# One sum of weight blocks in each group made by an adding DMA of the GpSimd queue instead of a VectorE add

## The chip, the cores and the metric

The kernel runs on one core of one Trainium2 chip. What counts is the device time of one execution in microseconds (us); lower is better. The kernel before is given as the median of three timed runs, and one more execution was taken by the hardware profiler. Engines are named as in the profile: PE is TensorE, PEld its weight loads, DVE is VectorE, ACT is ScalarE, POOL is GpSimd, and SP is SyncE, which here does nothing but issue DMAs.

## The reference

Attention with a tanh cap on the scores, and two feed-forward layers behind it, on 4 x 448 = 1792 tokens:

```python
scores = scale * np.matmul(q, k.transpose(0, 1, 3, 2))   # 4 batches, 12 heads, 448 x 64
scores = cap * np.tanh(scores / cap)
attn = softmax(scores) @ v                               # -> x, 1792 x 768
h = x @ moe_w_in                                         # 768 -> 2048
x = (h - np.tanh(h)) @ moe_w_out                         # 2048 -> 768
h = x @ moe2_w_in                                        # 768 -> 2048
out = (h * (1.0 / (1.0 + np.exp(-1.702 * h)))) @ moe2_w_out
```

The result is wanted with fp32 accuracy. TensorE multiplies in a shorter format (fp32r), so each fp32 operand is split into a high part (ACT casts it: `hi_act`, line L76) and a low part (DVE subtracts the high part from it: `lo_dve`, L88), and each product is made by three matmuls: high x high, high x low, low x high.

## The kernel before, in words

The tokens go through the feed-forward layers in two passes of two batches (896 tokens each). Both passes read the same weights, which lie in the chip's memory as blocks of 128 x 768 fp32 (384 KB): `single[n]` as plain fp32, and `kept[i]` already split. The first layer's input product of the second pass is `gemm_in(0)` (L779 to L791): 16 weight blocks, each with two spans of columns (512 and 384) and 18 matmuls a span. Behind each span `g_cubic` (L676) makes h - tanh h with a handful of ACT and DVE instructions (L680 to L698).

The first layer's output product of the second pass is `gemm_out_seven` (L833, matmuls at L854), and the second layer's input product is `gemm_in_seven` (L913, matmuls at L938). They split the matrices in two halves each way and make seven block products instead of eight, so some of their weight blocks are sums of blocks: s1 = r21 + r22, s3 = r21 - r11, s2 = r22 + r21 - r11, s4 = r12 - s2. These sums are made in the second pass while `gemm_in(0)` and then `gemm_out_seven` run, written to the chip's memory (`side_a`, `side_i`), and read back as weight blocks. The last stage is `gemm_rows_seven` (L971, matmuls at L997 and L1018).

The sums are made by two generators, in steps that end at each `yield`. `sums_a` (L333) has KQ = 4 groups of four blocks of 128 x 768; each group takes both buffers of `wd_p` (`four_of_pairs`), with four loads (L338), four adds (`add`, L313, through `first_sums`, L322) and four stores (L342). `sums_i` (L347) has KH = 8 groups, each with one buffer, two loads of 384 KB (L351), four adds on halves of 128 x 384, and two stores (L357). In the program of the trace their tiles are named `pair`.

The order of the work is that in which the program is written, with a scheduler that lets an instruction go ahead by its priority. `ahead(i)` is called once per weight block: it prepares the block that is used LEAD = 2 blocks later (`prepare` and `fetch`, loads at L258 and L283), and it advances the generators by `rate` steps, which carries over. In the second pass:

```python
side.extend((sums_a(), sums_i()))
rate[0] = 2.25
yield from gemm_in(0)
until("a")
rate[0] = 0.5
gemm_out_seven()
until("i")
gemm_in_seven()
```

All the loads and stores named so far are issued by SP, one after the other, in the order of the program. Weight blocks of `gemm_in(0)` come as two DMAs straight from `kept` (`wh` and `wl`, L283); those of `gemm_out_seven` and `gemm_in_seven` come as fp32 (`whole`, L258), ACT casts the high part, and DVE makes the low part `wl`. There are three buffers for split weight blocks. GpSimd has its last instruction before the second pass.

Of the kernel before, what the change touches and what calls it, by code (L numbers as in the profile page):

```python
# [15 lines left out]
ALU = mybir.AluOpType  # L16
# [21 lines left out]
def attention_moe_moe(ctx, tc, q, k, v, cap, w_in1, w_out1, w_in2, w_out2, out):  # L38
    nc = tc.nc
# [13 lines left out]
    HW = DM // 2  # L53
# [84 lines left out]
    A0, I0, R0 = KF, 2 * KF, 3 * KF  # L138
    KQ = KF // 4
# [80 lines left out]
    KH = KF // 2  # L220
    SEVEN_A = ("11", "s2", "12", "s3", "s1", "s4", "22")
    SEVEN_B = ("11", "21", "22", "t2", "t3", "t1", "t4")
    single = [dr_p.tile([P, WC], F32, name=f"single{n}") for n in range(NCH - A0)]
# [88 lines left out]
    def add(out, a, kind, b):  # L312
        nc.vector.tensor_tensor(out=out, in0=a, in1=b, op=kind)  # L313

    def four_of_pairs():
        slots = []
        for _ in range(2):
            t = wd_p.tile([P, WC, 2], U32, tag="wd", name="pair").rearrange("p w t -> p (w t)").bitcast(F32)
            slots += [t[:, :WC], t[:, WC:]]
        return slots  # L320

    def first_sums(r11, r12, r21, r22):  # L322
        add(r22, r21, ALU.add, r22)
        yield "s1", r22
        add(r21, r11, ALU.subtract, r21)
        yield "s3", r21
        add(r11, r22, ALU.subtract, r11)
        yield "s2", r11
        add(r12, r12, ALU.subtract, r11)
        yield "s4", r12  # L330
# [3 lines left out]
    def sums_a():  # L334
        for j in range(KQ):
            r = four_of_pairs()
            for n, t in enumerate(r):
                nc.sync.dma_start(out=t, in_=single[n * KQ + j])  # L338
                if n % 2:
                    yield  # L340
            for m, t in first_sums(*r):
                nc.sync.dma_start(out=side_a[m][j], in_=t)  # L342
                yield
        done.add("a")

    def sums_i():
        for j in range(KH):  # L347
            t = wd_p.tile([P, WC, 2], U32, tag="wd", name="pair").rearrange("p w t -> p (w t)").bitcast(F32)
            r = t[:, :WC], t[:, WC:]
            for n in range(2):  # L350
                nc.sync.dma_start(out=r[n], in_=single[I0 - A0 + n * KH + j])  # L351
            yield
            for n, _ in enumerate(first_sums(*(x[:, a:a + HW] for x in r for a in (0, HW)))):
                if n == 1:
                    yield
            for n in range(2):
                nc.sync.dma_start(out=side_i[j][n], in_=r[n])  # L357
            yield
        done.add("i")
# [745 lines left out]
    def moe(b0):  # L1105
        if b0 + NB == B:
# [8 lines that stand above are left out]
        else:  # L1115
            yield from gemm_in(0)
            gemm_out()
            plain[0] = True
            open_plain()
            side.append(sums_b())  # L1120
            rate[0] = 2.0
            yield from gemm_in(1)
        gemm_rows_seven(b0)
# [59 lines left out]
```

## Time and profile before

| what | value |
|---|---|
| time, median of 3 runs | 1097.28 us (1093.85 to 1097.44) |
| profiled execution, span of the trace | 1094.2 us |
| PE busy | 1081.3 us, 99% of the span |
| DVE busy | 929.8 us, 85% |
| ACT busy | 668.7 us, 61% |
| POOL busy | 59.1 us, 5% |
| DMA | 220.58 MB, mean 202 GB/s |
| `gemm_in(0)`, `gemm_out_seven`, `gemm_in_seven` of the second pass | 113.80, 104.16 and 104.16 us of PE |

The profiled execution is known by its span, from the first instruction to the last. The median of the three timed runs is 3.1 us above that span, and the fastest run 0.3 us below it. "Busy" counts instructions that compute; the time in which an engine issues DMAs or waits is not in it. The DMA share is the mean over the core's 16 DMA engines.

### The profile page before, as it was taken

Reading aid. Unit: us, or ns where it says so; the run is one execution under the profiler, and the core shown is the slowest. Engines: PE = TensorE matmul, PEld = TensorE weight load, DVE = VectorE, ACT = ScalarE, POOL = GpSimd, SP = SyncE. Lnnn points to the kernel's source line nnn. Section 1 sums busy time; section 2 is a strip of 40 time slices with the busy share of each in tenths; the row PEclk is TensorE's granted clock in tenths of the full one; section 3 lists DMA queues with packets and bytes.
Section 4 is the critical chain, followed back from the end, with each engine's and each line's share of the span. In section 5 each row is a group of like instructions: output and inputs, shape, how many; then the busy total and the mean of one; then the engine's idle time right before and its main releaser. Section 6 shows DMA issues by size and latency. Waiting matters only on the chain.

```text
span 1094.2 us, 16108 instructions
## 1 busy us (share of the span) xinstructions
PE 1081.3 (99%) x5579; PEld 887.0 (81%) x5579; DVE 929.8 (85%) x1467; ACT 668.7 (61%) x1022; POOL 59.1 (5%) x56
## 2 busy tenths in 40 slices
PE   9999998999999999999999999999999999999998
PEld 3333333688998888899899998889999999999998
DVE  4688999799997787889897885999999898889775
ACT  6898888799893433445245654767645554455453
POOL 0013443200000000000000000000000000000000
PEclk9999999999999999999999999999999999999999
DMA  6767786465537989889835768888555333333344
GB/s 142 206 187 199 192 234 192 148 209 173 188 116 265 318 305 332 292 287 313 285 110 170 227 201 276 313 287 291 183 192 176 107 123 102 102 110 107 119 144 142
DMA packets 156466, 220.58 MB, mean 202 GB/s; under 512 B 58672, under 2 KB 108640, under 8 KB 156384
## 3 DMA queue, kind: packets, MB, share of 16 engines
q1 hardware_dynamic: 155088, 218.94, 62.9%
q8 instruction: 44, 0.72, 0.3%
q10 hardware_dynamic: 1296, 0.61, 0.2%
q14 instruction: 38, 0.31, 0.1%
HBM read 160.83 MB, written 58.68 MB: 201 GB/s over the span
## 4 chain that ended last, share of the span: by engine, by line
PE 85%; DMA 6%; DVE 5%; ACT 2%; issue 2%; SPq 1%; ACTq 0%; DVEq 0%
PE ps_h L791 32%; PE ps_o L1018 15%; PE ps_h L938 10%; PE ps_y L854 10%; PE ps_pv L498 7%; PE ps_sc L457 5%; DMA wd<-in_moe_w_out_dram 4%; PE ps_o L997 3%; DVE wr L185 1%; DVE wd L175 1%; PE ps_qk L436 1%; PE ps_r L505 1%; PE ps_tl L467 1%; PE ps_y L816 1%; ACT wr L168 1%
## 5 line engine op out<-in xcount | busy, mean ns | idle before, releaser
L791 PE MATMUL ps_h<-xh,wh 128*128 128x384 f32 (+1 forms) x576 | 184.5, 365 | 0.3 <-ACT xh L76 0.3
L791 PE MATMUL ps_h<-xl,wh 128*128 128x384 f32 (+1 forms) x576 | 183.8, 364 | 0.0
L791 PE MATMUL ps_h<-xh,wl 128*128 128x384 f32 (+1 forms) x576 | 131.4, 362 | 0.1
L76 ACT CAST rh<-gr 128x384 fp32r<-128x384 f32 (+1 forms) x141 | 73.7, 528 | 82.8 <-PE ps_o L1018 36.4
L791 PEld LDWEIGHTS ps_h<-xh,wh 128*128 128x128 f32 x576 | 107.1, 188 | 13.8 <-ACT xh L76 1.0
L791 PEld LDWEIGHTS ps_h<-xl,wh 128*128 128x128 f32 x576 | 107.0, 188 | 11.9
L76 ACT CAST wh<-whole 128x768 fp32r<-128x768 f32 (+1 forms) x105 | 84.9, 810 | 50.4 <-PE ps_h L938 30.9
L791 PEld LDWEIGHTS ps_h<-xh,wl 128*128 128x128 f32 x576 | 104.6, 188 | 13.4 <-issue 1.4
L1018 PE MATMUL ps_o<-wl,rh 128*128 128x384 f32 x336 | 112.4, 335 | 1.1 <-DVE wl L88 1.1
L1018 PE MATMUL ps_o<-wh,rh 128*128 128x384 f32 x336 | 112.3, 334 | 0.0
L1018 PE MATMUL ps_o<-wh,rl 128*128 128x384 f32 x336 | 112.3, 334 | 0.0
L88 DVE TENSOR_TENSOR wl<-whole,wh 128x768 fp32r<-128x768 f32 (+1 forms) x105 | 96.5, 921 | 9.4 <-ACT wh L76 7.8
L168 ACT ACTIVATE wr<-wd 128x768 f32<-128x768 f32 x64 | 57.9, 909 | 69.6 <-DMA wd<-in_moe_w_out_dram 41.2
L88 DVE TENSOR_TENSOR rl<-gr,rh 128x384 fp32r<-128x384 f32 (+1 forms) x141 | 79.8, 573 | 13.7 <-ACT rh L76 12.9
L476 ACT ACTIVATE t<-ps_sc,tsc 128x896 f32<-128x896 f32 x72 | 70.0, 1008 | 26.6 <-PE ps_sc L457 26.6
L175 DVE TENSOR_SCALAR wd<-wd 128x768 uint16<-128x768 uint16 x57 | 59.5, 1044 | 24.9 <-ACT wr L168 24.7
L478 ACT ACTIVATE t<-t,cpos 128x896 f32<-128x896 f32 x72 | 72.5, 1044 | 0.4
L816 PE MATMUL ps_y<-gh,wh 128*128 128x512 f32 (+1 forms) x192 | 70.0, 365 | 1.6 <-DVE xl L88 1.4
L816 PE MATMUL ps_y<-gl,wh 128*128 128x512 f32 (+1 forms) x192 | 69.9, 364 | 0.0
L457 PE MATMUL ps_sc<-qk 64*128 64x448 f32 x288 | 68.2, 572 | 0.8 <-ACT qk L76 0.6
L498 PE MATMUL ps_pv<-t,rv 128*64 128x448 f32 x288 | 64.2, 551 | 3.9 <-ACT t L476 3.4
L1018 PEld LDWEIGHTS ps_o<-wl,rh 128*128 128x128 f32 x336 | 63.1, 188 | 1.6 <-DVE wl L88 1.4
(145 smaller groups left out, 2307.6 us busy)
## 6 DMA issues: line engine op xcount, KB each, us to landing
wd<-in_moe_w_in_dram SPq DMA_DIRECT2D x64, 384.0 KB
wd<-in_moe_w_out_dram SPq DMA_DIRECT2D x32, 768.0 KB
single<-wr SPq DMA_DIRECT2D x48, 384.0 KB
whole<-single SPq DMA_DIRECT2D x43, 384.0 KB
pair<-single SPq DMA_DIRECT2D x40, 384.0 KB
s<-pair SPq DMA_DIRECT2D x32, 384.0 KB
whole<-s SPq DMA_DIRECT2D x32, 384.0 KB
wh<-kept SPq DMA_DIRECT2D x25, 384.0 KB
```

The source lines that it names most:

```text
L76: pin(nc.scalar.copy(out=dst, in_=src))
L88: pin(nc.vector.tensor_tensor(out=dst, in0=src, in1=hi.bitcast(F32), op=ALU.subtract))
L175: pin(nc.vector.tensor_scalar(out=half[:, :, 2], in0=half[:, :, 1], scalar1=F64_LOW, scalar2=None, op0=ALU.mult))
L457: pin(nc.tensor.matmul(ps[:, j, :S], qk[a, kc], qk[a, :S], start=True, stop=True))
L476: pin(nc.scalar.activation(out=t, in_=ps[:, :, :S], func=AF.Tanh, scale=tsc))
L478: ins = pin(nc.scalar.activation(out=tt[g, c], in_=tt[g, c], func=AF.Exp, scale=cpos))
L498: pin(nc.tensor.matmul(ps[a, :S], w, t[:, j], start=(c == 0), stop=(c == KC - 1)))
L791: pin(nc.tensor.matmul(ps, w[:, kk, :], x[kk][:, a], start=(m == 0), stop=(m == len(seq) - 1)))
L816: nc.tensor.matmul(bank[e][:, :a1 - a0], w[:, kk, c], x[2 * j + kk][:, a0:a1], start=(j == 0 and m == 0), stop=(j == KF // 2 - 1 and m == ...
L854: nc.tensor.matmul(ps[e], w[:, kk, c], x, start=(k == 0 and m == 0), stop=(k == KH - 1 and m == 2))
L938: nc.tensor.matmul(ps, w, x, start=(m == 0), stop=(m == len(seq) - 1))
L1018: nc.tensor.matmul(ps[n], x[:, t], w[:, kk, :], start=(k == 0 and m == 0), stop=(k == KH - 1 and m == 2),)
```

## The change

The add that makes s1 is taken out of `first_sums`. In its place, a DMA that GpSimd issues reads r21 once more from the chip's memory and adds it to r22 in the tile where r22 has just been loaded. In `sums_a` this DMA has a step of its own: one `yield` more per group. In `sums_i` it shares the step of the loads. The other three sums of a group stay on DVE, and the stores stay on SP.

```diff
     def first_sums(r11, r12, r21, r22):
-        add(r22, r21, ALU.add, r22)
         yield "s1", r22
         add(r21, r11, ALU.subtract, r21)
         yield "s3", r21
@@ sums_a
                 nc.sync.dma_start(out=t, in_=single[n * KQ + j])
                 if n % 2:
                     yield
+            nc.gpsimd.dma_start(out=r[3], in_=single[2 * KQ + j], accum_op=ALU.add)
+            yield
             for m, t in first_sums(*r):
                 nc.sync.dma_start(out=side_a[m][j], in_=t)
                 yield
@@ sums_i
             for n in range(2):
                 nc.sync.dma_start(out=r[n], in_=single[I0 - A0 + n * KH + j])
+            nc.gpsimd.dma_start(out=r[1][:, HW:], in_=single[I0 - A0 + KH + j][:, :HW], accum_op=ALU.add)
             yield
```

So 4 DVE adds of 128 x 768 and 8 of 128 x 384 go, and 4 DMAs of 384 KB and 8 of 192 KB come on the GpSimd queue. The steps of `sums_a` go from 24 to 28.

The order of the SP queue around the first group of `sums_a`, before (`pair` is a block of the group in its buffer, `s1_0` to `s4_0` are the group's sums in memory, `wh` and `wl` are weight blocks of `gemm_in(0)`):

```order
L338 DMA pair_6514<-single12_198 128x768
L283 DMA wh_6573<-kept3_173 128x768
L283 DMA wl_6574<-kept3_173 128x768
L283 DMA wh_6645<-kept4_174 128x768
L342 DMA s1_0_234<-pair_6514 128x768
L342 DMA s3_0_242<-pair_6514 128x768
L283 DMA wl_6646<-kept4_174 128x768
L342 DMA s2_0_238<-pair_6513 128x768
L342 DMA s4_0_246<-pair_6513 128x768
L283 DMA wh_6717<-kept5_175 128x768
L283 DMA wl_6718<-kept5_175 128x768
```

The same place on SP after the change:

```order
L337 DMA pair_6514<-single12_198 128x768
L283 DMA wh_6573<-kept3_173 128x768
L283 DMA wl_6574<-kept3_173 128x768
L283 DMA wh_6643<-kept4_174 128x768
L283 DMA wl_6644<-kept4_174 128x768
L343 DMA s3_0_242<-pair_6514 128x768
L343 DMA s1_0_234<-pair_6514 128x768
L343 DMA s2_0_238<-pair_6513 128x768
L283 DMA wh_6715<-kept5_175 128x768
L283 DMA wl_6716<-kept5_175 128x768
L343 DMA s4_0_246<-pair_6513 128x768
```

The stores of the first group stand later against the weight loads by one or two places; the store of s1 now stands behind that of s3, and ahead of the weight block `kept5`.

The order on DVE at the third group of `sums_a`, before, with the semaphores that each instruction waits on (DMAHW: a DMA of SP, DMASW: a DMA of GpSimd); the rows with `pair` are the four adds of the group, s1, s3, s2 and s4:

```order
L313 TENSOR_TENSOR pair_6872<-pair_6872 128x768 [waits DMAHW6_49,DMAHW3_49,DMAHW0_49]
L695 TENSOR_TENSOR g_t_6974<-g_v_6988,g_t_6974 128x512 [waits DVE_49,Activation_49]
L313 TENSOR_TENSOR pair_6872<-pair_6871,pair_6872 128x768 [waits DMAHW1_49,DVE_49]
L697 SCALAR_TENSOR_TENSOR gr6_4258<-gr6_4258,g_t_6974 128x512 [waits DVE_49,Activation_49]
L681 TENSOR_TENSOR g_far_7006<-ps_h_6978,g_t_7005 128x384 [waits Activation_49]
L698 COPY_PREDICATED gr6_4258<-g_m_6989,g_far_6975 128x512 [waits DVE_49]
L313 TENSOR_TENSOR pair_6871<-pair_6872,pair_6871 128x768 [waits DMAHW4_49]
L695 TENSOR_TENSOR g_t_7005<-g_v_7029,g_t_7005 128x384 [waits DVE_49,Activation_49]
L313 TENSOR_TENSOR pair_6871<-pair_6871 128x768 [waits DMAHW2_49,DVE_49]
```

The same place on DVE after the change (s3, s2, s4):

```order
L313 TENSOR_TENSOR pair_6940<-pair_6939,pair_6940 128x768 [waits DMAHW5_49,DMAHW7_49,DMAHW1_49,DMAHW0_49]
L697 TENSOR_TENSOR g_t_6970<-g_v_6984,g_t_6970 128x512 [waits DVE_49,Activation_49]
L699 SCALAR_TENSOR_TENSOR gr6_4258<-gr6_4258,g_t_6970 128x512 [waits DVE_49,Activation_49]
L700 COPY_PREDICATED gr6_4258<-g_m_6985,g_far_6971 128x512 [waits DVE_49]
L683 TENSOR_TENSOR g_far_7002<-ps_h_6974,g_t_7001 128x384 [waits Activation_49]
L697 TENSOR_TENSOR g_t_7001<-g_v_7023,g_t_7001 128x384 [waits DVE_49,Activation_49]
L313 TENSOR_TENSOR pair_6939<-pair_6940,pair_6939 128x768 [waits DMAHW4_49,DMAHW3_49,DMASW2_49]
L699 SCALAR_TENSOR_TENSOR gr6_4258<-gr6_4258,g_t_7001 128x384 [waits DVE_49,Activation_49]
L88 TENSOR_TENSOR rl6_4289<-gr6_4258,rh6_4288 128x448 [waits Activation_49]
L700 COPY_PREDICATED gr6_4258<-g_m_7024,g_far_7002 128x384 [waits DVE_49]
L313 TENSOR_TENSOR pair_6939<-pair_6939 128x768 [waits DMAHW2_49]
```

The add of s1 is gone; the add of s2 waits for the adding DMA (DMASW2) and stands five instructions behind that of s3. In the first group of `sums_a` six instructions stand between the two.

The order on SP at the loads of the eighth and last group of `sums_i` (`single23` and `single31`), before, where they stand among the weight loads in the middle of `gemm_out_seven`:

```order
L357 DMA s31_6_263<-pair_8186 128x768
L351 DMA pair_8386<-single23_209 128x768
L357 DMA s24_6_262<-pair_8186 128x768
L258 DMA whole_8096<-s3_3_245 128x768
L351 DMA pair_8386<-single31_217 128x768
L258 DMA whole_8124<-s1_0_234 128x768
```

The same loads after the change, among the weight loads of the beginning of `gemm_in_seven` (`s31_1`, `single25`):

```order
L258 DMA whole_8714<-s31_1_253 128x768
L352 DMA pair_8618<-single23_209 128x768
L352 DMA pair_8618<-single31_217 128x768
L258 DMA whole_8752<-single25_211 128x384
L258 DMA whole_8784<-single18_204 128x768
L359 DMA s31_7_265<-pair_8618 128x768
L359 DMA s24_7_264<-pair_8618 128x768
```

They have moved behind the whole of `gemm_out_seven`, with the group's adds on DVE. On PE nothing moves.

## Rows read from the trace of the kernel before

**Rows 1.** The page: the span, and each engine's busy time and instructions.

```profile
span 1094.2 us, 16108 instructions
PE 1081.3 (99%) x5579; PEld 887.0 (81%) x5579; DVE 929.8 (85%) x1467; ACT 668.7 (61%) x1022; POOL 59.1 (5%) x56
...
POOL 0013443200000000000000000000000000000000
```

**Rows 2.** The chain that ended last, in order: start us, length us, what.

```profile
660.22 4.01 DMA wl<-kept
...
664.27 113.80 PE ps_h L791 x564
778.07 104.16 PE ps_y L854 x504
882.23 104.16 PE ps_h L938 x504
```

**Rows 3.** Stretches: length, busy PE, PEld, DVE, ACT, POOL, PE clock, DMA share, GB/s.

```profile
680.00:700.00 20.00, 20.00 (x102) 18.09 (x101) 19.04 (x32) 14.39 (x25) 0.00 (x0) 1.00 0.87 302
700.00:720.00 20.00, 20.00 (x101) 18.09 (x101) 17.32 (x29) 13.38 (x24) 0.00 (x0) 1.00 0.83 291
720.00:740.00 20.00, 20.00 (x99) 17.80 (x98) 19.27 (x34) 14.13 (x25) 0.00 (x0) 1.00 0.89 310
740.00:760.00 20.00, 20.00 (x100) 17.82 (x99) 20.00 (x40) 13.16 (x22) 0.00 (x0) 1.00 0.92 312
760.00:780.00 20.00, 20.00 (x103) 18.28 (x102) 20.00 (x37) 15.71 (x26) 0.00 (x0) 1.00 0.61 216
780.00:800.00 20.00, 20.00 (x98) 18.18 (x97) 20.00 (x36) 11.07 (x20) 0.00 (x0) 1.00 0.54 182
```

**Rows 4.** DVE's groups from 664 to 850 us: busy us, mean ns, idle before.

```profile
L313 DVE TENSOR_TENSOR pair<-pair 128x384 f32<-128x384 f32 x32 | 17.2, 543 | 0.0
L313 DVE TENSOR_TENSOR pair<-pair 128x768 f32<-128x768 f32 x16 | 15.2, 950 | 1.4 <-DMA pair<-single 1.4
L698 DVE COPY_PREDICATED gr<-g_m,g_far 128x512 f32<-128x512 uint16 x16 | 11.8, 735 | 0.5
...
L697 DVE SCALAR_TENSOR_TENSOR gr<-gr,g_t 128x512 f32<-128x512 f32 x16 | 10.9, 684 | 0.6
```

**Rows 5.** Timeline of SP's queue: start us, time in the queue us, line, operation.

```profile
666.98 2.03 SPq L338 DMA_DIRECT2D pair<-single  x4
...
683.17 1.69 SPq L283 DMA_DIRECT2D wh<-kept  x1
...
705.81 0.42 SPq L338 DMA_DIRECT2D pair<-single  x1
```

**Rows 6.** Timeline of DVE, adds of sums_a; in brackets the wait ahead.

```profile
677.78 0.94 DVE L313 TENSOR_TENSOR pair<-pair 128x768 f32<-128x768 f32 x1
...
712.33 0.96 DVE L313 TENSOR_TENSOR pair<-pair 128x768 f32<-128x768 f32 x1 [1.44 <-DMA pair<-single]
```

**Rows 7.** Timeline of DVE, low parts of gemm_out_seven's second, third and fourth weight block.

```profile
771.61 0.94 DVE L88 TENSOR_TENSOR wl<-whole,wh 128x768 fp32r<-128x768 f32 x1
...
778.93 0.94 DVE L88 TENSOR_TENSOR wl<-whole,wh 128x768 fp32r<-128x768 f32 x1
...
782.96 0.94 DVE L88 TENSOR_TENSOR wl<-whole,wh 128x768 fp32r<-128x768 f32 x1
```

**Rows 8.** PE's waits from 600 us to the end: total us, times, longest.

```profile
PE ps_o L1018 <- DVE wl L88: 1.1, 1, 1.1
```

**Rows 9.** ACT's waits from 650 to 860 us: total us, times, longest.

```profile
ACT g_t L680 <- PE ps_h L791: 27.5, 19, 12.6
```

## The prediction

> **What bounds the kernel now.** I read the page first: PE is busy 1081.3 us of a span of 1094.2 us [rows 1], so at most 12.9 us could be won without taking work from PE, and the change takes none from it. Next comes the chain of waits, for the stages in which the sums are made: three PE blocks stand end to end, 664.27 + 113.80 = 778.07, and 778.07 + 104.16 = 882.23 [rows 2]. In such a chain a step from one PE block straight to the next means that PE went from matmul to matmul and nothing else came last. PE's own list of waits agrees: from 600 us to the end it has one wait, 1.1 us, and that one is in the last stage [rows 8]. The windows from 680 to 800 us show the same, 20.00 of 20 us PE at the full granted clock, and beside it a DVE that is nearly full: 19.04, 17.32, 19.27, and then 20.00 three times [rows 3]. So the change works on an engine that is close to the limit but not the limit. It can win nothing where PE never waits; the question is whether DVE, which now waits for GpSimd's DMAs, gets late enough that PE stops.
>
> **How late DVE may get.** DVE makes the low part `wl` of each weight block of `gemm_out_seven`, and PE needs it. That stage has 28 blocks in 104.16 us, 3.72 us a block [rows 2]. The third block is wanted at 778.07 + 2 x 3.72 = 785.51 and its `wl` was done at 778.93 + 0.94 = 779.87, 5.6 us early; the fourth at 789.23, done at 782.96 + 0.94 = 783.90, 5.3 us early [rows 2, 7]. These are the tightest margins, since before 778 the weights come split from memory and DVE has only h - tanh h to make; what DVE leaves undone there falls due from 778 on. So three things pay for waits before about 780 us:
> - the adds that go: 4 x 0.950 + 4 x 0.543 = 6.0 us [rows 4] (4 more of 0.543 go later);
> - DVE's idle time from 680 to 740: 0.96 + 2.68 + 0.73 = 4.4 us [rows 3];
> - the margin of `wl`: 5.3 us.
>
> Together 15.7 us. ACT is not the next limit: it waits for PE (27.5 us in 19 waits), not PE for it [rows 9].
>
> **What the change adds, part by part.**
> - *DVE.* 12 adds go, 4 x 0.950 + 8 x 0.543 = 8.1 us [rows 4]. Covered by PE, so worth nothing by themselves.
> - *The new wait.* The add for s2 now waits for the adding DMA, and this DMA may start only when r22 has landed. Queued behind the waiting add on DVE are the `g_cubic` instructions, and behind them `wl`. Let A be the time from the last load of a group having landed to the adding DMA having landed. No row shows such a DMA. From below, the one plain DMA of a block on the chain, 4.01 us [rows 2]. From above 13 us: a block load that was issued at 705.81 held DVE until 712.33 [rows 5, 6], 6.5 us in a busy stretch, and twice that for a DMA that has to read two sides and whose descriptors are written by a program. I take 4.0 + 1.3 = 5.3 us, the plain DMA and a second reading of 393 KB at the 312 GB/s that the busiest stretch moved [rows 3]; it is nearest to the row of 4.01 us, because that row is the same transfer between the same places.
> - *What of A is covered.* DVE doesn't go straight from the load to the s2 add: the order shows six instructions between the adds for s3 and s2 in the first group, five in the third. DVE's instructions there take 75.6 us over 135, 0.56 us each [rows 3]. First group: loads issued 666.98 to 669.01 [rows 5], landed by 675.5 with 6.5 us each; the first add of the group at 677.78 [rows 6], which with s1 gone is the place of s3, and six instructions end at 677.78 + 0.94 + 3.4 = 682.1, so 6.6 us of A are covered. Third group, the only one whose loads DVE waited for (1.44 us [rows 4, 6]): the last load landed at 712.33; DVE, no longer waiting, would do s3 at 710.9 and reach s2 at 710.9 + 0.95 + 2.8 = 714.6, so 2.3 us are covered. With A = 5.3 the stalls are 0 and 3.0 us, 1.5 in the mean.
> - *The sum.* At most eight adding DMAs are waited for before 780 us (four of `sums_a`, the first four of `sums_i`): 8 x 1.5 = 12 us against 15.7. The other four lie some 22 us apart in `gemm_out_seven`, and each has the margin of 5.3 us for itself. PE doesn't stop: 0 us.
> - *SP's queue.* The store of s1 now waits for the adding DMA, and behind it in SP's order stands the weight block `kept5`. It was issued at 683.17 [rows 5] and is wanted at 664.27 + 5 x 7.11 = 699.8 (16 blocks in 113.80 us [rows 2]), so with 6.5 us for its flight it may go at 693. The adding DMA of the first group has landed by 675.5 + 13 = 688.5 even at the upper bound. If that cover went, a block late by the difference would stop PE once. No effect.
> - *POOL.* It does nothing after the first quarter [rows 1]; its DMAs queue only behind one another.
> - *DMA.* Four more reads of 393 KB before 740 us are 1.57 MB, and each touches the destination too, so 5 us at 312 GB/s, up to 10 with the second side. The DMA share is 0.83 to 0.92 from 680 to 760 [rows 3], which leaves 0.13 + 0.17 + 0.11 + 0.08 = 0.49 of 20 us, 9.8 us. It fits, narrowly.
> - *The moved group.* The eighth group of `sums_i` goes from the middle of `gemm_out_seven` to the first blocks of `gemm_in_seven`: its two loads, three adds (1.6 us) and two stores stand there beside that stage's own loads. Its sums are used last of all, a whole stage later. Between 780 and 800 the DMA share has fallen to 0.54 [rows 3], so SP's loads have room. No effect, and if the cover is gone, one block late by about A - 5.3.
>
> The sum is the profiled span with nothing taken off or put on, 1094.2 us; the median of the shown runs lies 3.1 us above that span, so I forecast 1097 us.
>
> **The rivals.**
> - *DVE's waits stop PE (slower).* With the two covers the waits come to 8 x ((A - 6.6) + (A - 2.3)) / 2, a term below nothing counted as nothing. They pass 15.7 us at A = 6.2 us: that is the point from which it decides, and only 0.9 us above my value. For it speaks that block loads in this stretch took 6.5 us; with the second reading that is 7.8 us, which gives 4 x (1.2 + 5.5) - 15.7 = 11 us, so 1108 us. At the upper bound of 13 it gives 4 x (6.4 + 10.7) - 15.7 = 53 us, 1150 us. Against it: the load of 6.5 us had to get through SP's and the engines' queues together with three others, while the adding DMA goes out alone.
> - *The adding DMA doesn't start while DVE works (slower).* Then nothing of A is covered, since it begins only when DVE stands still for it: 8 x 5.3 - 15.7 = 27 us, 1124 us. It decides if DVE's instructions there hold GpSimd off. What DVE runs in this stretch are two-operand adds, predicated copies and the like [rows 4], and POOL's own work shows no such hold, because it has none there [rows 1]. The Trainium skill ("SBUF — State Buffer", section "SBUF: two separate sides") describes such a hold: descriptors of a GpSimd DMA can't be written while VectorE runs an instruction in a mode that takes the port pair which the two share. It names copies and the like for it, and no run here shows it.
> - *SP or the moved group makes a weight block late (slower).* One stop, at the price of an adding DMA that lands at 13 instead of 5.3: 8 us, 1105 us. For it: a store that waits stands ahead of weight loads. Against it: the margin of 4.5 us at the upper bound, worked out above.
> - *DVE's relief reaches PE (faster).* Were PE's blocks stretched by waits too short to be listed, 6.0 us less of DVE work could give up to 6 us, 1091 us. Against it: full windows and a single wait of 1.1 us [rows 3, 8].
>
> That the change doesn't do what it says is excluded by the order: the adds are gone and the DMAs are there.
>
> **How the numbers follow.** About 0.5% (5.5 us) is what a measurement of this kernel can tell from no change. My forecast, no change, has 0.68: it holds for A up to 6.2 us, and some way above it, since the first few us past it lie within 0.5%. The rivals: waits on DVE 0.20, the held-off DMA 0.05, a late weight block 0.03, so slower 0.28; DVE's relief, faster, 0.04. Low end 1092, the fastest run shown (1093.85) less 2 us for what of the relief may reach PE. High end 1110: it takes in the wait rival up to A = 8 and the late block; beyond it lie the upper half of the first rival and the second, together some 0.17.
>
> **What would show it.** Right: the three PE blocks are again 113.8, 104.2 and 104.2 us, PE has no wait between 664 and 1000 us, and DVE shows idle time before the `pair` adds of about 1.5 us a group, released by a GpSimd DMA. Also right: DVE's busy time is 8 us less, the new DMAs take 4 to 6 us from issue to landing. Wrong: PE waits for `wl` near 780 us, or for a `kept` block near 700 us; DVE stands for over 2 us at each s2 add; or the adding DMAs take over 6.2 us.

## The result and the profile after

The changed kernel takes 1104.42 us (median of 4 runs, 1102.09 to 1105.47), the kernel before 1095.73 us beside it (median of 4). The ratio is 1.0085, with a 95% interval of 1.0059 to 1.011: slower by 0.85%, 8.7 us. The time lies in the range given (1092 to 1110), but the forecast was no change, and that was wrong.

The page of the profiled execution, with its span and busy times (compare [rows 1]):

```profile
span 1103.6 us, 16143 instructions
PE 1080.6 (98%) x5579; PEld 888.2 (80%) x5579; DVE 922.9 (84%) x1455; ACT 666.5 (60%) x1022; POOL 69.6 (6%) x68
```

PE and ACT do the same work, DVE is busy 6.9 us less, and the span is 9.4 us longer: PE stands. The windows say where (columns as in [rows 3]: length, busy PE, PEld, DVE, ACT, POOL, PE clock, DMA share, GB/s):

```profile
680.00:700.00 20.00, 20.00 (x100) 17.89 (x99) 14.93 (x24) 13.19 (x24) 0.87 (x1) 1.00 0.86 266
700.00:720.00 20.00, 20.00 (x102) 18.09 (x101) 15.74 (x25) 11.93 (x22) 0.86 (x1) 1.00 0.85 286
720.00:740.00 20.00, 20.00 (x102) 18.07 (x101) 14.39 (x23) 10.45 (x19) 0.86 (x1) 1.00 0.74 251
740.00:760.00 20.00, 18.00 (x81) 15.48 (x80) 14.44 (x26) 9.42 (x17) 1.61 (x2) 0.91 0.84 246
760.00:780.00 20.00, 18.70 (x91) 16.18 (x90) 15.87 (x32) 9.78 (x17) 1.85 (x3) 1.00 0.85 269
780.00:800.00 20.00, 14.36 (x61) 11.68 (x60) 20.00 (x36) 15.09 (x27) 1.73 (x2) 0.91 0.71 210
800.00:820.00 20.00, 19.80 (x96) 17.67 (x95) 20.00 (x36) 11.08 (x21) 0.00 (x0) 1.00 0.47 151
```

Where before PE was busy 20.00 of 20 in each, it now loses 2.00 + 1.30 + 5.64 + 0.20 = 9.1 us, 3.3 of it before 780 us and 5.8 behind. (That 9.1 is so close to the 9.4 us of the span is chance: the last section has the rest of the sum.) DVE, nearly full before, has 4 to 6 us of idle time in each window up to 780 and is full only then.

PE's waits from 600 us to the end (total us, times, longest), where before there was one of 1.1 us [rows 8]:

```profile
PE ps_y L856 <- DVE wl L88: 3.1, 4, 1.0
PE ps_y L856 <- ACT wh L76: 2.8, 2, 2.1
PE ps_h L793 <- DMA wh<-kept: 2.6, 2, 2.0
PE ps_o L1020 <- DVE wl L88: 1.5, 1, 1.5
PE ps_h L793 <- DVE pair L313: 0.7, 1, 0.7
PE ps_o L999 <- DVE wl L88: 0.6, 1, 0.6
```

So there are two kinds of stop: in `gemm_in(0)` (L793) PE waits mostly for weights that come straight from memory (`wh<-kept`), which no DVE instruction makes, and in `gemm_out_seven` (L856) for the two parts of a weight block that ACT and DVE make. ACT's part (`wh`) is late by DVE too: up to 800 us ACT has no wait for the load of a `whole` block, but its casts stand in order behind its instructions of `g_cubic`, and these wait for DVE 26.8 + 17.6 us, against 11.3 + 2.8 before:

```profile
ACT g_m L696 <- DVE gr L700: 26.8, 13, 4.8
ACT g_v L693 <- DVE g_t L697: 17.6, 10, 5.2
```

DVE's groups of `pair` adds from 664 to 850 us (busy, mean ns, idle before; compare [rows 4]):

```profile
L313 DVE TENSOR_TENSOR pair<-pair 128x768 f32<-128x768 f32 x12 | 11.4, 954 | 14.4 <-DMA pair<-single 14.4
L313 DVE TENSOR_TENSOR pair<-pair 128x384 f32<-128x384 f32 x21 | 11.4, 548 | 7.6 <-DMA pair<-single 7.6
```

DVE now waits 22.0 us ahead of these adds, against 1.4 before. For the third group, GpSimd's queue and then DVE (start us, us, engine, line, operation, wait ahead):

```profile
717.04 0.86 POOL L340 DMA_DIRECT2D pair<-single  x1 [20.53 <-DMA wl<-kept]
```

```profile
722.87 0.96 DVE L313 TENSOR_TENSOR pair<-pair 128x768 f32<-128x768 f32 x1 [3.76 <-DMA pair<-single]
```

The adding DMA is issued at 717.04, and DVE's add for s2, which waited 3.76 us for it, starts at 722.87, 5.8 us later. (The bracket on GpSimd's row names a weight load; where a wait is for several semaphores, the profile names one of them. The load that the adding DMA waits for has landed at 716.4.) The view of DMA issues (count, KB each, median us from issue to landing) has 5.5 and 4.8 us for the two sizes:

```profile
pair<-single POOLq DMA_DIRECT2D x4, 384.0 KB, 5.5
pair<-single POOLq DMA_DIRECT2D x8, 192.0 KB, 4.8
```

Of the 22.0 us, 19.2 lie in six waits for adding DMAs (1.9 to 4.1 us each), and 2.8 in two waits for plain loads that came late.

The chain that ended last (start us, length us) is no longer PE's alone, as in [rows 2]. From 717 to 790 us it runs through the groups of sums: an adding DMA, the store of a sum, the loads of a next group, its adding DMA, and at last DVE's `wl`:

```profile
717.04 5.80 DMA pair<-single
...
726.20 2.69 DMA s<-pair
728.95 7.67 DMA pair<-single
...
738.15 5.19 DMA pair<-single
...
753.72 5.88 DMA pair<-single
...
767.39 3.50 DMA s<-pair
771.32 6.99 DMA pair<-single x2
...
789.83 0.88 DVE wl L88
790.75 4.82 PE ps_y L856 x15
...
893.56 102.14 PE ps_h L940 x504
```

The rows at 717.04, 738.15 and 753.72 start with GpSimd's issues: they are adding DMAs.

SP's queue stands too. First its longest waits from 662 to 800 us before (total us, times, longest). Those at L258 and L283, ended by a weight buffer's becoming free, are the time by which SP is early with weight loads, 41.3 us in all; this is called SP's lead below. The others are stores that wait for DVE's adds:

```profile
SPq L258 <- DVE wl L88: 21.5, 7, 6.3
SPq L342 <- DVE pair L313: 21.0, 15, 4.1
SPq L283 <- PE ps_h L791: 19.8, 14, 5.4
SPq L357 <- DVE pair L313: 14.5, 9, 2.8
```

The same stretch after the change:

```profile
SPq L343 <- DMA pair<-single: 23.2, 4, 6.7
...
SPq L359 <- DMA pair<-single: 14.7, 3, 6.5
...
SPq L283 <- PE ps_h L793: 6.4, 4, 4.9
...
SPq L258 <- DVE wl L88: 5.8, 1, 5.8
```

The stores of the sums (L343, L359) now hold SP 37.9 us for the adding DMAs, and still 25.0 us for DVE (19.2 and, at L359, 5.8), where before they held it 35.5 us for DVE. The lead falls from 41.3 to 12.2 us.

### The profile page after: what moved, and what is told of

It reads as the page before. It is cut to its first block, busy times and chain, and to the rows that moved or that the text cites. A ratio compares the mean times of both kernels' runs of the same rounds, so it can differ in the third digit from the quotient of the medians.

```text
span 1103.6 us, 16143 instructions
## 1 busy us (share of the span) xinstructions
PE 1080.6 (98%) x5579; PEld 888.2 (80%) x5579; DVE 922.9 (84%) x1455; ACT 666.5 (60%) x1022; POOL 69.6 (6%) x68
## 4 chain that ended last, share of the span: by engine, by line
PE 81%; DMA 8%; DVE 5%; ACT 2%; issue 2%; SPq 1%; DVEq 0%; ACTq 0%; POOLq 0%
PE ps_h L793 26%; PE ps_o L1020 14%; PE ps_h L940 9%; PE ps_y L856 9%; PE ps_pv L500 7%; PE ps_y L818 5%; PE ps_sc L459 5%; DMA pair<-single 3%; PE ps_o L999 2%; DMA wd<-in_moe_w_out_dram 2%; PE ps_qk L438 1%; PE ps_r L507 1%; PE ps_tl L469 1%; DVE wd L175 1%; ACT t L478 1%
## 5 line engine op out<-in xcount | busy, mean ns | idle before, releaser
L793 PE MATMUL ps_h<-xh,wh 128*128 128x384 f32 (+1 forms) x576 | 185.3, 367 | 3.3 <-DMA wh<-kept 2.6
L793 PE MATMUL ps_h<-xl,wh 128*128 128x384 f32 (+1 forms) x576 | 184.7, 366 | 0.0
L793 PE MATMUL ps_h<-xh,wl 128*128 128x384 f32 (+1 forms) x576 | 131.3, 362 | 0.0
L793 PEld LDWEIGHTS ps_h<-xh,wh 128*128 128x128 f32 x576 | 107.7, 189 | 17.4 <-DVE g_t L697 2.3
L793 PEld LDWEIGHTS ps_h<-xl,wh 128*128 128x128 f32 x576 | 107.5, 189 | 12.2
L793 PEld LDWEIGHTS ps_h<-xh,wl 128*128 128x128 f32 x576 | 104.7, 188 | 12.9 <-issue 1.4
L175 DVE TENSOR_SCALAR wd<-wd 128x768 uint16<-128x768 uint16 x57 | 59.6, 1045 | 23.4 <-ACT wr L168 23.2
L856 PE MATMUL ps_y<-rh,wl 128*128 128x448 f32 x168 | 62.6, 373 | 3.1 <-DVE wl L88 3.1
```

The costliest lines, as they stand in the source:

```text
L175: pin(nc.vector.tensor_scalar(out=half[:, :, 2], in0=half[:, :, 1], scalar1=F64_LOW, scalar2=None, op0=ALU.mult))
L793: pin(nc.tensor.matmul(ps, w[:, kk, :], x[kk][:, a], start=(m == 0), stop=(m == len(seq) - 1)))
L856: nc.tensor.matmul(ps[e], w[:, kk, c], x, start=(k == 0 and m == 0), stop=(k == KH - 1 and m == 2))
```

## The experiments

Two theories stood at first. D: DVE's standing makes the low parts `wl` of the weight blocks late. S, later widened to C: the adding DMA is a serial link in the chain of a group (loads, adding DMA, adds, stores, next loads into the same buffer), and SP, which issues that chain in order with the weight loads, gets late with these. The kernel before was timed beside each run on the same chip; its medians were 1094.0 to 1094.3 us. "Stop" is what PE's busy time lacks in the profile, in `gemm_in(0)` and in `gemm_out_seven`; "DVE waits" are its idle times ahead of `pair` adds; "backlog" is explained below the table. The medians are of 4 to 12 executions, while stops, waits and backlog are those of one profiled execution of each kernel, so the two need not agree to the last us.

| run | median us | ratio (95%) | stop, `gemm_in(0)` | stop, `gemm_out_seven` | DVE waits for `pair`, to 800 us | backlog |
|---|---|---|---|---|---|---|
| the change | 1104.42 | 1.0085 (1.0059 to 1.011) | 3.3 | 5.8 | 22.0 | 14.8 |
| stores on GpSimd | 1116.02 | 1.0215 (1.0188 to 1.0243) | 14.0 | 3.9 | 31.6 | 11.0 |
| s2 first | 1101.02 | 1.0067 (1.0048 to 1.0085) | 1.5 | 3.5 | 13.1 | 10.7 |
| s2 first, s1's store on GpSimd | 1108.53 | 1.0132 (1.0107 to 1.0157) | 6.1 | 2.2 | 20.4 | 9.2 |
| no adding DMA | 1093.87 | 1.0001 (0.9987 to 1.0015) | 0.0 | 0.0 | 4.2 | 2.8 |
| `sums_a` only | 1095.71 | 1.0014 (0.9995 to 1.0033) | 0.0 | 3.5 | 12.2 | 11.2 |
| `sums_i` only | 1092.75 | 0.9983 (0.9969 to 0.9997) | 0.7 | 1.4 | 8.4 | 7.6 |
| slower steps | 1102.04 | 1.007 (1.005 to 1.0089) | 0.0 | 5.4 | 11.6 | 10.7 |
| early adding DMA | 1106.98 | 1.012 (1.01 to 1.0141) | 8.4 | 3.5 | 23.2 | 10.8 |
| plain DMA | 1099.13 | 1.0059 (1.0036 to 1.0082) | 0.0 | 3.2 | 11.8 | 10.4 |
| s2 first, slower steps | 1099.96 | 1.0056 (1.0043 to 1.0069) | 0.6 | 4.7 | 13.5 | 10.7 |
| s2 later, slower steps | 1095.44 | 1.0019 (1.0001 to 1.0037) | 0.0 | 3.8 | 8.8 | 9.3 |
| before, slower steps | 1093.84 | 1.0002 (0.9992 to 1.0012) | 0.0 | 0.0 | 3.1 | 2.9 |

The backlog is the time from the first matmul of `gemm_out_seven` to the end of the last tanh of `g_cubic`, so it says how far ACT and DVE are behind PE when the next stage begins. The rows are ACT's and PE's timelines. Before, 778.23 + 0.48 - 777.91 = 0.8 us:

```profile
778.23 0.48 ACT L680 ACTIVATE g_t<-ps_h 128x384 f32<-128x384 f32 x1
```

```profile
777.91 0.36 PE L854 MATMUL ps_y<-rh,wh 128*128 128x448 f32 x1
```

In the changed kernel, 796.29 + 0.48 - 781.98 = 14.8 us:

```profile
796.29 0.48 ACT L682 ACTIVATE g_t<-ps_h 128x384 f32<-128x384 f32 x1
```

```profile
781.98 0.36 PE L856 MATMUL ps_y<-rh,wh 128*128 128x448 f32 x1
```

**Stores on GpSimd.** All stores of the sums leave SP:

```diff
-                nc.sync.dma_start(out=side_a[m][j], in_=t)
+                nc.gpsimd.dma_start(out=side_a[m][j], in_=t)
-                nc.sync.dma_start(out=side_i[j][n], in_=r[n])
+                nc.gpsimd.dma_start(out=side_i[j][n], in_=r[n])
```

> The change with the stores of all sums issued by GpSimd instead of SP: SP no longer stands for an adding DMA ahead of weight loads, DVE's s2 adds wait as in the change. Theory D (DVE's waits for the adding DMAs, about 19 us before 780 us, are what makes the weight blocks of gemm_out_seven late): PE loses again about 9 us from 740 to 800 us, time about 1104 us. Theory S (SP's queue, held 5 to 7 us by each store of s1, issues the weight loads late): the waits of PE vanish, time about 1096 us. Both in half: about 1100 us.

It was slower than either theory had it, 1116 us. SP's waits from 662 to 800 us, and PE's longest:

```profile
SPq L352 <- DMA s<-pair: 50.8, 6, 13.6
SPq L337 <- DMA s<-pair: 32.3, 6, 12.3
```

```profile
PE ps_h L793 <- DMA wh<-kept: 14.0, 3, 6.2
```

SP no longer stands at a store; it stands 83 us at the loads of the next group, until the stores have landed and the buffer is free. Moving the wait to another queue made the chain longer and SP later. The stop of 14.0 us is all for weights straight from memory, which SP issues late. S in its narrow form (the store is the trouble) fell; C, the length of the chain, came in its place.

**s2 first.** By the code s3 is r11 - r21 (the words ahead of the prediction gave it with the other sign), so s2 = r22 - s3, and it can be made before anything is added to r22:

```diff
-        add(r11, r22, ALU.subtract, r11)
+        add(r11, r22, ALU.subtract, r21)
...
             for m, t in first_sums(*r):
                 nc.sync.dma_start(out=side_a[m][j], in_=t)
                 yield
+            nc.gpsimd.dma_start(out=r[3], in_=single[2 * KQ + j], accum_op=ALU.add)
+            yield
+            nc.sync.dma_start(out=side_a["s1"][j], in_=r[3])
+            yield
```

In `sums_i` likewise, the adding DMA between the adds and the two stores; `first_sums` no longer yields s1.

> s2 is made as r22 - s3, which is the same sum, from r22 before anything is added to it; the adding DMA and the store of s1 come behind, the store still on SP. DVE then waits for no adding DMA, SP still does, once a group. Theory D: no PE wait from 664 to 1000 us, time 1094 to 1098 us. Theory S: the weight loads are late as in the change, PE loses most of 9 us, time 1101 to 1105 us.

DVE waits for no adding DMA, and yet 13.1 us, now for the loads of the next group, which SP issues late. D expected nothing left and is missed. S has the time, at the lower edge of its 1101 to 1105 us, but not the way: the stops lie mostly in `gemm_out_seven` (3.5 of 5.0 us), not at weights from memory.

**s2 first, s1's store on GpSimd.** As above, with the store of s1 (and in `sums_i` the one that holds s3 and s1) behind the adding DMA on GpSimd's queue:

```diff
-            nc.sync.dma_start(out=side_a["s1"][j], in_=r[3])
+            nc.gpsimd.dma_start(out=side_a["s1"][j], in_=r[3])
```

> As the version with s2 from s3, and the store of s1 is issued by GpSimd behind its own adding DMA: neither DVE nor SP waits for an adding DMA. Both theories D and S: no PE wait, DVE 8 us less busy, time 1094 to 1098 us, like the kernel before. A third theory, that the added DMA traffic itself delays the weight loads, expects 1100 us or more here too.

A miss for both: 1108.5 us. SP's waits for a buffer go to 29.6 + 17.3 = 46.9 us (18.3 in the change), by the same way as with all stores on GpSimd. The third theory, added traffic, had 1100 us or more and is not refuted by this run; what speaks against it is the run with s2 later below, which has all the adding DMAs and their bytes and takes 1095.4 us.

**No adding DMA.** The two added DMAs are taken out of the change, and its order stays:

```diff
-            nc.gpsimd.dma_start(out=r[3], in_=single[2 * KQ + j], accum_op=ALU.add)
-            nc.gpsimd.dma_start(out=r[1][:, HW:], in_=single[I0 - A0 + KH + j][:, :HW], accum_op=ALU.add)
```

> The change without its adding DMAs: the sum s1 is left out (r22 stands for it), nothing waits, the order of the change (one step more per group, the eighth group behind gemm_out_seven) stays. If the order alone costs something, over 1098 us; if only the DMAs and their waits cost, 1094 to 1097 us, with 8 us less DVE work and no gain from it, since PE has no wait to lose.

As expected: the order costs nothing, and the DVE work that goes gives nothing. It shows one thing more. Take the stretch from DVE's first `g_far` of `gemm_in(0)` to its last, the one behind the last tanh. DVE's busy time in it is the fourth number after the stretch's length (PE, PEld, DVE); before:

```profile
666.60:780.40 113.80, 113.80 (x568) 102.42 (x567) 106.31 (x182) 80.32 (x137) 0.00 (x0) 1.00 0.82 286
```

Without the adds and without the DMAs:

```profile
664.49:779.82 115.33, 115.33 (x575) 103.82 (x574) 104.93 (x181) 79.94 (x137) 0.00 (x0) 1.00 0.81 280
```

In the changed kernel:

```profile
665.04:798.53 133.49, 124.55 (x595) 109.51 (x594) 104.84 (x178) 79.18 (x139) 8.67 (x10) 0.97 0.83 262
```

Four adds of 128 x 768 and four of 128 x 384, 6.0 us, are gone from this stretch, and yet DVE's work in it is only 1.4 to 1.5 us less: in the new order other work, of `gemm_out_seven`, stands ahead of the last `g_far` in their place. And with the waits DVE needs 19.7 us longer for the stretch (133.5 against 113.8), for 20.6 us more of waits ahead of `pair` adds (22.0 against 1.4): nearly every us of waiting is a us later.

**One half of the change at a time.** `sums_a` only, then `sums_i` only; the other keeps its DVE add of s1:

```diff
-    def first_sums(r11, r12, r21, r22):
+    def first_sums(r11, r12, r21, r22, one=False):
+        if one:
+            add(r22, r21, ALU.add, r22)
         yield "s1", r22
```

> Only sums_a uses the adding DMA (4 of 384 KB, 28 steps as in the change); the groups of sums_i keep the DVE add. Theory C (the chain of a group - loads, adding DMA, adds, stores, then the next loads into the same buffer - gets longer by some 6 us for each adding DMA, and SP, which issues it in order with the weight loads, loses the slack of about 41 us that it had from 662 to 800 us): four links cost SP about 24 us, less than its slack; the loss is below half of the change's, 1094 to 1099 us. Theory D (DVE's standing): 11.6 us of waits against 15.7 us, no loss, 1094 to 1097 us.

> Only sums_i uses the adding DMA (8 of 192 KB), in the order of the kernel before (24 steps in sums_a). Its groups are those that run into the first weight blocks of gemm_out_seven, where most of PE's loss lies (5.6 of 9.1 us from 780 to 800 us). Theory C: more than half of the change's loss, 1098 to 1102 us. Theory D: 7.6 us of waits against a margin of over 10, no loss, 1094 to 1097 us.

Each half alone costs next to nothing in time, 0.14% and -0.17%, though PE stops 3.5 and 2.2 us in the profiles (that of `sums_a` only is of an execution 3.0 us above its median). Nearly no stop is left in `gemm_in(0)`: with four links, or eight short ones, SP keeps a lead of 24.5 and 29.8 us. The loss does not add up from the halves. That it is what goes beyond a slack which both share is a reading, not tested further. For `sums_i` alone Theory C had expected 1098 us or more, and was wrong; Theory D had no loss for either and is near in time, but not in its reason: PE stops with waits of 12.2 and 8.4 us, below the 15.7 us that were to pay for them.

**Slower steps.** The change with its groups further apart:

```diff
-            rate[0] = 2.25
+            rate[0] = 1.75
...
-            rate[0] = 0.5
+            rate[0] = 0.875
```

> The change with its steps spread: 1.75 instead of 2.25 a block in gemm_in(0), so that the 28 steps of sums_a fill its 16 blocks (a group every 28 us instead of 22), and 0.875 instead of 0.5 in gemm_out_seven for those of sums_i. The adding DMAs, their waits on DVE and their bytes stay. Theory C: a group's chain, some 22 us, fits into its time, SP's slack comes back, PE has no wait of note before 780 us, time 1094 to 1098 us. If the wait itself or the traffic is the cost: about 1102 to 1105 us, like the change.

Half a hit. The stops in `gemm_in(0)` are gone, all of them, as C has it. The time stays at 1102 us by a stop of 5.4 us at the start of `gemm_out_seven`, where the backlog is 10.7 us, after waits of 11.6 us. Here SP's lead is back at 29.0 us. So there are two causes, and this run shows DVE's without SP's. The time alone would also fit the expectation's other case, the traffic; against that stands the run with s2 later, again.

**Early adding DMA.** r22 is loaded first, and its adding DMA issued straight behind it:

```diff
-            for n, t in enumerate(r):
-                nc.sync.dma_start(out=t, in_=single[n * KQ + j])
-                if n % 2:
+            for n in (3, 2, 1, 0):
+                nc.sync.dma_start(out=r[n], in_=single[n * KQ + j])
+                if n == 3:
+                    nc.gpsimd.dma_start(out=r[3], in_=single[2 * KQ + j], accum_op=ALU.add)
+                if n % 2 == 0:
                     yield
```

> The change with r22 loaded first and its adding DMA issued straight behind it, so that it runs beside the loads of the other blocks (in sums_i: the second block first). Theory C: a group's chain is shorter by 2 to 6 us, the loss falls by more than half, 1095 to 1099 us, and DVE's waits for adding DMAs fall below 8 us. If the bytes of the adding DMAs are the cost: as the change, 1103 to 1105 us.

A miss: 1107 us. Beside the other loads the adding DMA lands later (for the blocks of 384 KB a median of 7.8 us from its issue instead of 5.5; for those of 192 KB 4.8 as before), and SP's stores wait 34.4 us for it instead of 23.2. The flight got longer, and what it lost ate what the early issue had won.

**Plain DMA.** GpSimd's DMA copies r21 over r22 (the sum s1 is left out):

```diff
-            nc.gpsimd.dma_start(out=r[3], in_=single[2 * KQ + j], accum_op=ALU.add)
+            nc.gpsimd.dma_start(out=r[3], in_=single[2 * KQ + j])
```

> The change with GpSimd's DMAs copying r21 over r22 instead of adding it (the sum s1 is left out, r21 stands for it); every wait and the order stay. If the reading of the destination and the adding are what makes a link of the chain long: the DMAs land in about 4 us instead of 5.5 after their issue, DVE's waits fall by some 10 us and the loss by more than half, 1095 to 1099 us. If any serial DMA would do it: flights and waits as in the change, 1102 to 1106 us.

The two sizes, from issue to landing:

```profile
pair<-single POOLq DMA_DIRECT2D x4, 384.0 KB, 4.0
pair<-single POOLq DMA_DIRECT2D x8, 192.0 KB, 3.3
```

With the adding a DMA lands 1.5 us later, for either size. With links that much shorter DVE's waits fall from 22.0 to 11.8 us and the stops in `gemm_in(0)` are gone; the start of `gemm_out_seven` still stops 3.2 us. About four tenths of the loss go (5.1 us are left of 8.7), less than the half that was expected.

**s2 first with slower steps, and s2 later with slower steps.** The first joins two edits above; the second puts the add of s2 in `sums_a` behind a later instruction of `g_cubic` on DVE:

```diff
+        with ExitStack() as behind:
+            for ins in (cubics[-back:][:1] if back else []):
+                behind.enter_context(tc.issue_after(ins))
-        add(r11, r22, ALU.subtract, r11)
+            add(r11, r22, ALU.subtract, r11)
```

`cubics` collects the instructions of L698, `back` is 1, 3, 6 and 9 for the four groups.

> s2 from s3 (DVE waits for no adding DMA) together with the slower steps (1.75 and 0.875 a block, so that a group's chain fits into its time). If the loss has the two causes that the runs so far point to, DVE's backlog at the start of gemm_out_seven and SP's late weight loads in gemm_in(0), both are gone: no PE wait of over 1 us from 664 to 800 us, 1093 to 1097 us. If PE still loses 4 to 6 us at the start of gemm_out_seven, neither wait is its cause.

> The change with the slower steps, and in sums_a the add of s2 put 7 to 15 instructions behind that of s3 on DVE instead of 5 to 13, so that DVE arrives when the adding DMA has landed. With the slower steps alone DVE waited 11.6 us and PE lost 5.4 us, all of it at the start of gemm_out_seven. If DVE's waits cause that: waits below 5 us, PE loses below 2 us, 1095 to 1099 us. If not: PE loses 5 us again, 1101 to 1103 us.

The first missed: DVE waited 13.5 us, not for adding DMAs but for loads, since s2 first puts all adds close behind the loads, and the stop was again 4.7 us. By the letter of the expectation ("If PE still loses 4 to 6 us ... neither wait is its cause") that would clear both; but the wait had not gone, so the run doesn't decide it. The second is a partial hit. Its time is 1095.4 us, against 1102.0 us with the slower steps alone, so putting the add of s2 later takes most of the loss away. That it does so by a shorter wait of DVE is likely but not shown: in the profile, whose execution took 4.3 us more than the median, DVE still waited 8.8 us and PE stopped 3.8 us, more than was expected. PE's waits for the blocks:

```profile
PE ps_y L861 <- DVE wl L88: 2.3, 3, 0.9
...
PE ps_y L861 <- ACT wh L76: 1.4, 1, 1.4
```

**Before with slower steps**, the control (1.5 instead of 2.25, 0.875 instead of 0.5):

```diff
-            rate[0] = 2.25
+            rate[0] = 1.5
```

> Control: the kernel before with steps of 1.5 a block in gemm_in(0) (its 24 steps fill the 16 blocks) and 0.875 in gemm_out_seven, no adding DMA. Nothing to lose and nothing to win: 1092 to 1097 us, PE without a wait. If it is slower by over 4 us, the spread itself (sums_i among the first blocks of gemm_out_seven) costs, and the runs with slower steps have to be read against it.

No change, as expected, so the steps themselves cost nothing.

**What the runs have in common.** Put side by side are the backlog less the margin of `wl` of 5.3 us from the prediction, the stop in `gemm_out_seven`, SP's lead from 662 to 800 us, and the stop in `gemm_in(0)`, in the order of the lead:

| run | backlog - 5.3 | stop, `gemm_out_seven` | SP's lead | stop, `gemm_in(0)` |
|---|---|---|---|---|
| before, slower steps | below 0 | 0.0 | 46.8 | 0.0 |
| before | below 0 | 0.0 | 41.3 | 0.1 |
| s2 later, slower steps | 4.0 | 3.8 | 34.8 | 0.0 |
| no adding DMA | below 0 | 0.0 | 31.6 | 0.0 |
| plain DMA | 5.1 | 3.2 | 30.5 | 0.0 |
| `sums_i` only | 2.3 | 1.4 | 29.8 | 0.7 |
| slower steps | 5.4 | 5.4 | 29.0 | 0.0 |
| s2 first, slower steps | 5.4 | 4.7 | 26.7 | 0.6 |
| `sums_a` only | 5.9 | 3.5 | 24.5 | 0.0 |
| stores on GpSimd | 5.7 | 3.9 | 17.1 | 14.0 |
| early adding DMA | 5.5 | 3.5 | 13.7 | 8.4 |
| the change | 9.5 | 5.8 | 12.2 | 3.3 |
| s2 first, s1's store on GpSimd | 3.9 | 2.2 | 11.0 | 6.1 |
| s2 first | 5.4 | 3.5 | 10.7 | 1.5 |

In `gemm_out_seven` PE stops in the runs with a backlog of 7.6 us and more and in no other (none lies between 2.9 and 7.6), and never by more than the backlog less the margin. In `gemm_in(0)` it stops 1.5 us or more in the five runs with a lead of 17.1 us or less, and at most 0.7 us where the lead is 24.5 us or more. So backlog and lead tell which stage stops; how long, they tell only roughly, and within the five runs the stop doesn't follow the lead.

## Why the prediction was wrong

- **The bound, and that nothing is to be won: right.** PE stood end to end before, and DVE without the 12 adds gave nothing (1.0001).
- **"Three things pay for waits": the step that failed.** I set 6.0 us of removed adds, 4.4 us of idle time and the margin of 5.3 us against the waits, 15.7 us in all. Only the margin paid in full. Of the 6.0 us, 4.5 were taken by other work that moved up, as the three stretches above show, and DVE's idle time did not close either: where it waits for ACT's tanh it was 4.9 + 2.4 us ahead of `g_far` before, and 4.2 + 2.4 after. The plainest sign are the runs that had waits as forecast, 12 us or about it: with 8.4 to 12.2 us (`sums_i` only, s2 later, slower steps, plain DMA, `sums_a` only) PE stopped 1.4 to 5.4 us in `gemm_out_seven`, where the sum has 0. What decides is a backlog somewhere between 2.9 and 7.6 us, and the margin of 5.3 us lies there.
- **The mean stall of 1.5 us: too small.** Six of the eight adding DMAs held DVE, 19.2 us in all, 2.4 us in the mean, and 2.8 us came on top for loads that SP issued late: 22.0 us against the 12 of the sum. Part of it is a cover read wrongly. For the first group I put the add of s3 at 677.78, where s1 had been; but s3 doesn't need r22 as s1 did, so it went at 674.61, and DVE came to s2 at 679.1 instead of 682.1, with 2.9 us to wait instead of 0:

```profile
674.61 0.95 DVE L313 TENSOR_TENSOR pair<-pair 128x768 f32<-128x768 f32 x1
...
682.02 0.96 DVE L313 TENSOR_TENSOR pair<-pair 128x768 f32<-128x768 f32 x1 [2.93 <-DMA pair<-single]
```

- **A, the time from the loads to the adding DMA's landing: somewhat too small.** I took 5.3 us. The flight alone is 5.5 and 4.8 us (medians of the two sizes), and GpSimd issues it some 0.6 us after the last load has landed (716.4 and 717.04 in the third group): 6.1 and 5.4 us together (6.4 in that third group). In the mean that is still below the 6.2 us at which, by the sum, the first rival decides, so A alone doesn't turn the forecast.
- **"SP's queue. No effect": wrong.** I looked at the first group alone, which indeed had time. But the same hold returns with every group, SP's lead of 41 us fell to 12, and three groups later the weights from memory were late: 2.6 us of PE's stops. What the slower steps took away is this part.
- **The moved group: right**: PE has no stop in `gemm_in_seven`. That DMA traffic fits is borne out too: from 680 to 820 us no window of 20 us reaches a DMA share above 0.86 (before, 0.92), and s2 later, with all the adding DMAs, takes 1095.4 us.
- **The rival that happened is the first**, DVE's waits stop PE, forecast at 1108 us for A of 7.8 us and given 0.20, with the late weights of the third rival, given 0.03, beside it. That 1108 us lies near the 1104.4 measured is luck: A was 6.1 us at most by the medians, and the rival too let 15.7 us pay. The second, that the adding DMA doesn't start while DVE works, did not happen: GpSimd issued two of them between 780 and 800 us in 0.86 us each, while DVE was busy 20.00 of 20. The hold that the Trainium skill describes ("SBUF — State Buffer", section "SBUF: two separate sides") is not seen in that window. The Trainium skill says on that page, in "Who interferes with whom", that a `tensor_tensor` has no two-port mode and was seen not to stall a DMA; 26 of DVE's 36 instructions in that window are `tensor_tensor`, and as far as two issues can show it the trace agrees.

How far each cause goes in the change, by PE's stops: 5.8 us at the start of `gemm_out_seven`, by DVE's backlog, directly and through ACT, and 3.3 us in `gemm_in(0)`, mostly SP's late loads. That the two are shared so is argued from who released PE and ACT. DVE's part without SP's is shown in another kernel (slower steps); SP's without DVE's in none, since in the run with the largest stop in `gemm_in(0)`, stores on GpSimd, DVE waits too (31.6 us) and PE stops 3.9 us in `gemm_out_seven`. The two are not independent either: stores that wait for DVE's adds hold SP (25.0 us), and loads that SP issues late hold DVE (2.8 us).

## What to carry to other kernels

An operation that leaves a busy engine for a DMA leaves a wait behind. On DVE here, which runs its instructions in the program's order, 20.6 us more of waits made a stretch 19.7 us longer, and the 6.0 us freed by the operation paid 1.5 us at most, because the order had given the rest to other work. So weigh the wait against the margin of the next consumer, and count freed time only where the new order shows it free. A DMA that works on a buffer also lengthens that buffer's round (loads, DMA, adds, stores, next loads), and a queue that carries this round together with urgent loads hands the delay on to them group by group, so look at the last group and not at the first.

## What was not expected of the hardware

- The adding DMA took 5.5 and 4.8 us (medians) from issue to landing for 384 and 192 KB, the plain copy in its place 4.0 and 3.3: 1.5 us more for either size.
- PE's stops cost clock on top. After the stop of 2.0 us at 747 to 749 us of the changed kernel, and again after those at 786 to 791 us, the granted clock was 0.50 for two us, that is 1.2 instead of 2.4 GHz (from 750 to 752, and here):

```profile
792.00:794.00 2.00, 2.00 (x7) 1.74 (x6) 2.00 (x5) 1.52 (x3) 0.00 (x0) 0.50 0.92 207
```

With the windows of two us on either side (0.92 and 0.73; 0.66 and 0.99) that costs 1.7 us at full clock each time, 3.4 us in all. The sum of the profile is then: stops 9.1 and clock 3.4, less 2.0 by the next point, less 1.2 by which PE came earlier to `gemm_in(0)` (660.09 against 661.26), together 9.3 of the 9.4 us.

- After some of the stops PE ran a little faster than before them. In `gemm_in_seven` (895 to 985 us) the kernel before has 438 matmul records and the changed one 445 in the same 90 us, both at a granted clock of 1.00:

```profile
895.00:985.00 90.00, 90.00 (x438) 81.74 (x437) 76.18 (x137) 45.96 (x83) 0.00 (x0) 1.00 0.35 105
```

```profile
895.00:985.00 90.00, 90.00 (x445) 83.41 (x445) 79.12 (x141) 45.70 (x82) 0.86 (x1) 1.00 0.44 132
```

It was so in the profiles of the change, of `sums_i` only, of the stores on GpSimd, of the early adding DMA and of s2 first with slower steps, and it gives back about 2 us in that stage (102.14 us in the chain above instead of the 104.16 of [rows 2]), which may be why `sums_i` alone comes out 0.17% faster than the kernel before. What sets it was not tried and stays open.
